# Attention scores in four quarters of TensorE, q and k loaded first, and a written order for the first block of a fused attention and expert kernel

## The chip, the cores and the metric

The kernel runs on one core of a Trainium2 chip. The metric is device time in microseconds (us). Before the change it is 997.73 us, the median of 3 runs (997.62 to 998.29).

## The reference

Three stages follow each other; all arrays are float32.

```
scores = q_c @ k_c^T / 8          # 4 batches x 8 heads x 9 chunks of 64 tokens, head size 64
attn   = softmax(scores)          # with the row's maximum taken off first
x      = (attn @ v_c) -> [2304 tokens, 512]
h      = x @ w_in;  g = h * clip(h + 3, 0, 6) / 6;  x2 = g @ w_out        # d_ff = 2048
logits = x2 @ w_gate;  noisy = logits + log1p(exp(x2 @ w_noise)) * noise  # 8 experts, top 2
out    = sum over the token's two experts of  weight * (relu(x2 @ w1[e]) @ w2[e])   # 1024 wide
```

## The kernel before

Tokens are cut into 18 tiles of 128; a tile holds two chunks of 64 tokens for all 8 heads. The middle stage runs in five blocks of 4, 4, 4, 3 and 3 tiles (`BT`, L28), and in each block over 16 units of 128 hidden channels (`U1`). Of a unit, `mlp_s1` (L294) makes the first product, 12 matmuls (L270), each weight and input being split into a high and a low part and three of the four products taken; `mlp_act` (L301) and `mlp_lo` (L309) make `g` (ScalarE L304, VectorE L305, ScalarE L306, VectorE L311); `mlp_o` (L313) makes the second product, 3 matmuls per tile (L279), one unit later. The experts' stage follows with 64 more units.

**Ticks.** TensorE's order is written by hand: after every 4 matmuls of a first product and every 3 (a tile) of a second one, `tick` (L259) runs the work that was put down for that number with `at`. A unit has 7 ticks in blocks of 4 tiles, 6 in blocks of 3. Attention of block b+1 and the gate of block b-1 are placed into block b in this way (L688 to L709). From block 0 on, the order of VectorE, ScalarE and SyncE (SP, which issues the loads) is left to a scheduler that works with its own estimates of durations.

**Weights.** Those of the middle stage arrive as 64-bit numbers. A unit has two halves (first and second product), 32 halves in all. `load64(s)` (L123) loads 512 KB for a half; `conv_u` (L133) takes three VectorE operations (L142, L143, L144) to put the float32 bits together; `conv_hi` (L148) makes the high part on ScalarE (L152), `conv_lo` (L154) the low part on VectorE (L159). They run during block 0, two halves per unit (L641). From half 14 on, three buffers are in use: `conv_u(s)` issues the load of half s+3.

**Attention of a tile.** `att_sc` (L164) makes the scores in 16 matmuls of 64 x 64 (32 instructions, L171): rows of the array hold one of two groups of heads (`r`), and each writes the same half of the output partitions, into one bank of PSUM. `att_mx` (L174) takes the maximum (L177) and subtracts it (L183), or, with `acts`, only scales it (L181) for `att_e` (L186), which then takes one exp per head with the maximum as bias and the sum as an extra output (L191), else one exp for all (L193). `att_n` (L195) sums if needed (L198), and multiplies by the inverse (L199, L200, L201). `att_pt` (L210) transposes on TensorE (L214), `att_at` copies (L218), `att_xo` (L225) makes the products with v (L235) in four quarters of the array and two banks, `att_hi` and `att_lo` split the result into the block's input, `Xa` or `Xb` (ScalarE L245, VectorE L248).

**PSUM.** `pairs` (L53) are two tiles of two banks each: pair 0 holds banks "p6" and "p7", pair 1 "p2" and "p5". Scores go to p6, transposes to p7, value products to the left half of both banks of pair 0, the gate's `gate_t`, `gate_m`, `gate_r` (L336 to L360) to p7. The second product uses p0, p1, p2 and p5.

**Before block 0** (L602 to L620) the order on TensorE, VectorE and ScalarE is written by hand: attention of tiles 0 to 3 and the first two halves of weights, with `keep_warm` (L545) matmuls on constants between. The loads are issued in the order tile 0 (three parts), tiles 1 to 3, halves 0 to 6 (L557). `constants` (L563) and `table_init` (L573) set up small tables, the latter at unit 6 of block 0.

## Time and profile before

| | |
|---|---|
| median of 3 runs | 997.73 us (997.62 to 998.29) |
| profiled execution: its own time, span | 996.98 us, 995.2 us |
| TensorE (PE) busy | 955.8 us, 96% of the span |
| its weight loads (PEld) busy | 811.2 us, 82% |
| VectorE (DVE) busy | 433.6 us, 44% |
| ScalarE (ACT) busy | 338.9 us, 34% |
| GpSimd (POOL) busy | 141.7 us, 14% |
| loads and stores | 99.47 MB, 100 GB/s on average |

A profile is one execution. Engines are PE (matmuls), PEld (their weight loads, beside PE), DVE, ACT, POOL and SP; L171 is line 171 of the kernel; `pair<-arena` is what an instruction writes and reads, by the program's names; x32 counts instructions. Matmuls are pipelined, and the ends that a profile gives them are modelled: how long a group takes on PE is better read from its start to the start of the next group. PEclk is the granted share of TensorE's clock.

### The profile page before, as it was taken

The numbers are of one execution on the slowest core, as the hardware profiler recorded it, in microseconds if no ns is written. First come the engines' busy times: TensorE is split into PE (matmuls) and PEld (weight loads), VectorE is DVE, ScalarE is ACT, GpSimd is POOL, SyncE is SP. The second block draws the span as 40 slices with busy tenths as digits, with TensorE's granted clock in tenths as the row PEclk, the third lists the DMA queues.
The fourth block names the chain that finished last, engine by engine and source line by source line (L and its number), as shares of the span: only waits on it lengthen the run. The fifth ranks groups of instructions, "written<-read, shape, count | busy, mean of one in ns | idle before, by whom it ended". The sixth has DMA issues, their size and how long they took to land.

```text
span 995.2 us, 14562 instructions
## 1 busy us (share of the span) xinstructions
PE 955.8 (96%) x5980; PEld 811.2 (82%) x5980; DVE 433.6 (44%) x863; ACT 338.9 (34%) x661; POOL 141.7 (14%) x129
## 2 busy tenths in 40 slices
PE   6898799999999999999999999999999999999995
PEld 4676687777777788878988899898998999899894
DVE  4999824344433434336542543434333343422221
ACT  4454433323333233335541433333333333321110
POOL 0000000000200020032103321301313130130311
PEclk8899899999999999999999999999999999999998
DMA  9536312011651021013541663644636354340422
GB/s 341 161 129 216 130 32 75 32 33 32 231 189 36 1 85 33 22 33 86 179 139 22 170 154 95 130 110 114 131 106 138 96 127 117 85 54 22 53 25 33
DMA packets 37196, 99.47 MB, mean 100 GB/s; under 512 B 9984, under 2 KB 10368, under 8 KB 37120
## 3 DMA queue, kind: packets, MB, share of 16 engines
q1 hardware_dynamic: 27008, 77.43, 24.0%
q0 software_dynamic: 10112, 21.02, 11.8%
q8 instruction: 49, 0.80, 0.3%
q14 instruction: 27, 0.22, 0.1%
HBM read 75.15 MB, written 23.28 MB: 99 GB/s over the span
## 4 chain that ended last, share of the span: by engine, by line
PE 87%; DVE 8%; DMA 2%; issue 1%; ACT 1%; POOL 0%; SPq 0%; DVEq 0%; ACTq 0%; POOLq 0%
PE h L270 41%; PE acc L279 21%; PE pair L279 19%; PE pair L453 2%; DMA raw<-in_w1u_dram 2%; DVE u L144 1%; DVE u L143 1%; PE pair L340 1%; PE pair L171 1%; DVE u L142 1%; PE pair L235 1%; DMA lead<-in_qkv_dram 1%; DVE g L311 1%; DVE r L305 1%; PE pair L349 1%
## 5 line engine op out<-in xcount | busy, mean ns | idle before, releaser
L279 PE MATMUL acc<-w,g 128*128 128x512 f32 x960 | 262.4, 398 | 2.5 <-DVE g L311 2.3
L270 PE MATMUL h<-Xa,w 128*128 128x320 f32 (+3 forms) x1344 | 251.7, 337 | 1.8 <-DVE Xa L248 1.7
L279 PE MATMUL pair<-w,g 128*128 128x512 f32 x864 | 235.3, 400 | 0.8 <-ACT at L341 0.8
L270 PEld LDWEIGHTS h<-Xa,w 128*128 128x128 f32 x1344 | 217.0, 189 | 22.7 <-DVE Xa L248 2.0
L279 PEld LDWEIGHTS acc<-w,g 128*128 128x128 f32 x960 | 174.3, 188 | 35.2 <-DVE g L311 3.2
L279 PEld LDWEIGHTS pair<-w,g 128*128 128x128 f32 x864 | 161.5, 190 | 38.3 <-ACT at L341 1.3
L119 DVE TENSOR_TENSOR w<-raw,w 128x1024 fp32r<-128x1024 f32 x64 | 78.4, 1226 | 132.6 <-ACT w L118 132.4
L470 DVE SCALAR_TENSOR_TENSOR g<-h,g 128x320 fp32r<-128x320 f32 (+2 forms) x128 | 62.5, 489 | 154.8 <-ACT g L469 145.4
L469 ACT ACTIVATE g<-h 128x320 fp32r<-128x320 f32 (+2 forms) x128 | 56.0, 438 | 191.6 <-PE h L270 186.4
L270 PE MATMUL h<-Xe,w 128*128 128x320 f32 (+1 forms) x672 | 110.2, 315 | 0.0
L270 PE MATMUL h<-Xb,w 128*128 128x384 f32 (+1 forms) x480 | 106.6, 366 | 0.0
L305 DVE SCALAR_TENSOR_TENSOR r<-r,h 128x512 f32<-128x512 f32 (+1 forms) x80 | 50.6, 632 | 126.4 <-ACT r L304 117.5
L270 PEld LDWEIGHTS h<-Xe,w 128*128 128x128 f32 x672 | 103.5, 188 | 2.5
L118 ACT ACTIVATE w<-raw 128x1024 fp32r<-128x1024 f32 x64 | 67.8, 1060 | 104.8 <-PE pair L279 97.1
L304 ACT ACTIVATE r<-h,b 128x512 f32<-128x512 f32 (+1 forms) x80 | 51.7, 646 | 151.9 <-PE h L270 150.7
L426 POOL DMA_INDIRECT table<-pay,slot x36 | 36.6, 1017 | 413.1 <-DVE slot L423 403.6
L270 PEld LDWEIGHTS h<-Xb,w 128*128 128x128 f32 x480 | 85.6, 188 | 11.1 <-issue 0.8
L443 POOL DMA_INDIRECT xr<-x2d,tab x40 | 39.3, 981 | 271.0 <-PE pair L453 252.1
L491 POOL DMA_INDIRECT out_dram<-arena,tab x40 | 63.1, 1576 | 88.0 <-DVE arena L488 69.7
L311 DVE TENSOR_TENSOR g<-r,g 128x512 fp32r<-128x512 f32 (+1 forms) x80 | 50.9, 636 | 32.9 <-ACT g L306 31.6
L306 ACT ACTIVATE g<-r 128x512 fp32r<-128x512 f32 (+1 forms) x80 | 47.2, 590 | 44.1 <-DVE r L305 43.1
L152 ACT ACTIVATE w<-u 128x512 fp32r<-128x512 f32 x32 | 19.7, 635 | 22.8 <-DVE u L144 22.7
(134 smaller groups left out, 525.8 us busy)
## 6 DMA issues: line engine op xcount, KB each, us to landing
raw<-in_w2u_dram SPq DMA_DIRECT2D x64, 512.0 KB, 3.9
raw<-in_w1u_dram SPq DMA_DIRECT2D x24, 512.0 KB, 4.1
arena<-in_qkv_dram SPq DMA_DIRECT2D x14, 768.0 KB, 4.2
out_dram<-zero SPq DMA_DIRECT2D x4, 1536.0 KB
rawx<-in_w1u_dram SPq DMA_DIRECT2D x8, 512.0 KB, 13.4
x2d<-x SPq DMA_DIRECT2D x15, 256.0 KB
lead<-in_qkv_dram SPq DMA_DIRECT2D x3, 768.0 KB
x2d<-zero SPq DMA_DIRECT2D x1, 1536.0 KB
```

The lines of the kernel that those rows point to most:

```text
L118: nc.scalar.activation(w[:, 0], raw, AF.Copy)
L119: nc.vector.tensor_tensor(w[:, 1], raw, w[:, 0].bitcast(F32), op=ALU.subtract)
L270: nc.tensor.matmul(dst, w[:, a, kd * P:(kd + 1) * P], x[:, b, kd, t0:t0 + n], start=(k == 0), stop=(k == 3 * KD - 1))
L279: nc.tensor.matmul(acc[i], g[:, a, i * P:(i + 1) * P], w[:, b, DM:], start=(first and j == 0), stop=(last and j == 2))
L304: nc.scalar.activation(r, st["h", b], AF.Relu, bias=b3)
L305: nc.vector.scalar_tensor_tensor(r, r, 6.0, st["h", b], op0=ALU.min, op1=ALU.mult)
L306: nc.scalar.activation(st["g", b, u][:, 0], r, AF.Copy)
L311: nc.vector.tensor_tensor(g[:, 1], st["r", b], g[:, 0].bitcast(F32), op=ALU.subtract)
L443: nc.gpsimd.indirect_dma_start(out=xr, out_offset=None, in_=x2d[:rows], in_offset=bass.IndirectOffsetOnAxis(ap=st["tab", key][:, i, 0:1], ...
L469: nc.scalar.activation(g[:, 0, t0:t0 + n], h, AF.Relu)
L470: nc.vector.scalar_tensor_tensor(g[:, 1, t0:t0 + n], h, 0.0, g[:, 0, t0:t0 + n].bitcast(F32), op0=ALU.max, op1=ALU.subtract)
L491: s = nc.gpsimd.indirect_dma_start(out=out, out_offset=bass.IndirectOffsetOnAxis(ap=tab[:, i, 0:1], axis=0), in_=y, in_offset=None, comput ...
```

## The change

- `att_sc` writes chunk `c` to one half of the partitions and head group `r` to one of two banks, so that four quarters of the array are addressed in turn. Scores and value products use the left (or, for tiles 2 and 3, the right) half of both banks of a pair, transposes the right half of pair 0.
- `att_n` is divided: `att_r` (sum, inverse) and the multiplication; `att_ns` does the multiplication head by head on ScalarE. `conv_u` is divided into `conv_1` (L142, L143) and `conv_2` (L144 and the next load).
- q and k of tiles 0 to 3 are loaded first, then v with the weights. `constants` and `table_init` stand before the attention of tiles 0 to 3, whose order is written anew, with 27 warm matmuls in place of 30 and three halves of weights converted in place of two.
- Block 0 becomes `block0`, in which the order on TensorE, VectorE and ScalarE is written; a tile of attention is spread over four units (28 ticks), with the exps and the multiplications on ScalarE, four heads at a time.
- In blocks 1 to 3 the transposes come 6 ticks (5 in block 3) behind the scores instead of 11, the value products 4 ticks behind these as before, and the gate's three steps behind the value products instead of between scores and transposes.

The diff, cut to its core:

```diff
-    def load_tile(t, buf, parts=1):
-        n = 3 * DM // parts
-        for i in range(parts):
-            nc.sync.dma_start(buf[:, i * n:(i + 1) * n], qkv[:, t, i * n:(i + 1) * n])
+    def load_part(t, buf, i0, i1):
+        nc.sync.dma_start(buf[:, i0 * DM:i1 * DM], qkv[:, t, i0 * DM:i1 * DM])
+
+    def load_tile(t, buf, whole=True):
+        if whole:
+            load_part(t, buf, 0, 3)
...
-    def conv_u(s):
+    def conv_1(s):
         if s >= 2 * U1:
             return
         j, h = divmod(s, 2)
         if h == 0:
             st["w", "m", j] = wpool.tile([P, 2, 2 * DM], F32R, tag="w", bufs=U1, name="w")
-        raw = st.pop(("raw64", s)).rearrange("p (n c) -> p n c", c=2)
-        lo32, hi32 = raw[:, :, 0], raw[:, :, 1]
+        raw = st["raw64", s].rearrange("p (n c) -> p n c", c=2)
+        hi32 = raw[:, :, 1]
         u = work.tile([P, DM], I32, tag="x2", bufs=3, name="u")
         nc.vector.tensor_scalar(u, hi32, 3, 0x3fffffff, op0=ALU.logical_shift_left, op1=ALU.bitwise_and)
         nc.vector.scalar_tensor_tensor(u, hi32, -0x40000000, u, op0=ALU.bitwise_and, op1=ALU.bitwise_or)
+        st["u", s] = u
+
+    def conv_2(s):
+        if s >= 2 * U1:
+            return
+        lo32 = st.pop(("raw64", s)).rearrange("p (n c) -> p n c", c=2)[:, :, 0]
+        u = st["u", s]
         nc.vector.scalar_tensor_tensor(u, lo32, 29, u, op0=ALU.logical_shift_right, op1=ALU.bitwise_or)
-        st["u", s] = u
         load64(s + 7 if s < 10 else s + 3 if s >= 14 else -1)
...
-    def att_sc(t, tag):
+    def att_sc(t, pair=0, half=0):
         qt, kt, vt = st["qkv", t]
-        sc = bank(tag, [P, 8, 64], "sc")
-        for c in range(2):
-            for hp in range(KD):
+        sc = pairs[pair][:, :, half * 2 * P:(half + 1) * 2 * P].rearrange("p r (h k) -> p r h k", h=KD)
+        for hp in range(KD):
+            for c in range(2):
                 for r in range(2):
                     s = slice(r * 64, r * 64 + 64)
-                    nc.tensor.matmul(sc[s, c * KD + hp, :], qt[s, hp, c, :], kt[s, c, hp, :], start=True, stop=True)
+                    nc.tensor.matmul(sc[c * 64:c * 64 + 64, r, hp, :], qt[s, hp, c, :], kt[s, c, hp, :],
+                                     start=True, stop=True)
         st["sc", t] = sc
...
     def att_mx(t, acts):
         sc = st["sc", t]
-        mx = work.tile([P, 8, 1], F32, tag="mx", bufs=2, name="mx")
-        nc.vector.tensor_reduce(mx, sc, axis=AX.X, op=ALU.max)
+        mx = work.tile([P, 8, 1], F32, tag="mx", bufs=4, name="mx")
+        mx4 = mx.rearrange("p (r h) o -> p r h o", r=2)
+        nc.vector.tensor_reduce(mx4, sc, axis=AX.X, op=ALU.max)
         sm = (lead[t][:, 3 * DM:] if t < BT[0] else arena[:, 6]).rearrange("p (h k) -> p h k", h=8)
...
-    def att_e(t):
+    def att_e(t, heads=range(8)):
         sm, su, mx, acts = st["att", t]
-        sc = st.pop(("sc", t))
         if acts:
-            for h in range(8):
-                nc.scalar.activation(sm[:, h], sc[:, h], AF.Exp, scale=0.125, bias=mx[:, h], accum_out=su[:, h])
+            sc = st["sc", t]
+            for h in heads:
+                nc.scalar.activation(sm[:, h], sc[:, h // KD, h % KD], AF.Exp, scale=0.125, bias=mx[:, h],
+                                     accum_out=su[:, h])
...
+    def att_r(t):
         sm, su, mx, acts = st["att", t]
         if not acts:
             nc.vector.tensor_reduce(su, sm, axis=AX.X, op=ALU.add)
         nc.vector.tensor_scalar(su, su, 1e-9, None, op0=ALU.add)
         nc.vector.reciprocal(su, su)
+
+    def att_n(t):
+        att_r(t)
+        sm, su, mx, acts = st["att", t]
         nc.vector.tensor_tensor(sm, sm, su.to_broadcast([P, 8, 64]), op=ALU.mult)
-    def att_a(t, tag, acts):
-        att_sc(t, tag)
+    def att_ns(t, heads):
+        sm, su, mx, acts = st["att", t]
+        for h in heads:
+            nc.scalar.activation(sm[:, h], sm[:, h], AF.Copy, scale=su[:, h])
+
+    def att_a(t, acts):
+        att_sc(t)
...
-    def att_pt(t, tag):
+    def att_pt(t, tag=None):
         sm = st.pop(("att", t))[0].rearrange("p h k -> p (h k)")
-        pt = bank(tag, [P, KD, P], "pt")
+        if tag is None:
+            pt = pairs[0][:, :, 2 * P:].rearrange("p r (j n) -> p r j n", j=2)
+        else:
+            pt = bank(tag, [P, KD, P], "pt").rearrange("p (r j) n -> p r j n", r=2)
...
-    def att_xo(t, pair=0):
+    def att_xo(t, pair=0, half=0):
-                                         at[s, c * 2 + j, r * 64:r * 64 + 64], start=True, stop=True)
+                                         at[s, r * 2 + j, c * 64:c * 64 + 64], start=True, stop=True)
...
-    for c in [0, 1, 2, 3, 10, 11, 12, 13, 14, 15, 16]:
-        if c < 10:
-            load_tile(c, bufs[c], 3 if c == 0 else 1)
-        else:
-            load64(c - 10)
+    for t in range(4):
+        for i in ((0, 1), (1, 2)) if t == 0 else ((0, 2),):
+            load_part(t, bufs[t], *i)
+        load_tile(t, bufs[t], False)
+    load_part(0, bufs[0], 2, 3)
+    load_part(1, bufs[1], 2, 3)
+    load64(0)
+    load_part(2, bufs[2], 2, 3)
+    load_part(3, bufs[3], 2, 3)
+    for i in range(1, 7):
+        load64(i)
...
+    constants()
+    table_init()
+    LT = BT[0]
     with tc.manual_schedule(engines={nc.tensor.engine, nc.vector.engine, nc.scalar.engine}):
-        att_sc(0, "p0"), att_mx(0, True), att_e(0)
-        att_sc(1, "p1"), att_mx(1, True), att_e(1)
+        att_sc(0, 0, 0), att_mx(0, False), att_e(0)
+        att_sc(1, 1, 0), att_mx(1, True), att_e(1)
+        att_n(0)
+        keep_warm(1)
+        att_sc(2, 0, 1), att_mx(2, True)
+        att_sc(3, 1, 1), att_pt(0, "p0"), att_at(0, at_[0]), att_e(2)
+        att_mx(3, False), att_e(3)
+        att_n(1)
+        keep_warm(1)
+        att_xo(0, 0, 0), att_hi(0)
+        att_pt(1, "p1"), att_at(1, at_[1])
+        att_n(2), att_n(3)
         keep_warm(3)
-        att_n(0), att_pt(0, "p3"), att_at(0, at_[0])
-        att_sc(2, "p0"), att_mx(2, True)
-        keep_warm(3)
-        att_n(1), att_e(2), att_pt(1, "p3"), att_xo(0, 0), att_at(1, at_[1])
-        att_sc(3, "p1"), att_mx(3, False)
-        att_hi(0), att_e(3), att_xo(1, 1)
-        keep_warm(6)
-        conv_u(0)
-        att_lo(0), att_hi(1), conv_hi(0), att_n(2), att_n(3)
-        att_pt(2, "p3"), att_at(2, at_[0]), att_pt(3, "p3"), att_at(3, at_[1])
-        att_lo(1), att_xo(2, 0), att_xo(3, 1)
-        keep_warm(8)
-        conv_u(1), att_hi(2), conv_hi(1), att_hi(3)
-        conv_lo(0), conv_lo(1)
-        att_lo(2), att_lo(3)
-    constants()
-    LT = BT[0]
+        att_pt(2, "p0"), att_xo(1, 1, 0), att_pt(3, "p1")
+        conv_1(0), conv_2(0), conv_hi(0)
+        att_hi(1), att_lo(0)
+        att_at(2, at_[0]), att_at(3, at_[1])
+        att_xo(2, 0, 1), att_xo(3, 1, 1)
+        att_hi(2), att_hi(3)
+        att_lo(1), conv_lo(0), att_lo(2), att_lo(3)
+        keep_warm(12)
+        conv_1(1), conv_2(1), conv_hi(1)
+        conv_1(2), conv_2(2), conv_hi(2)
+        conv_lo(1), conv_lo(2)
...
-            if b == 0:
-                for s in (2 * u + 2, 2 * u + 3):
-                    conv_u(s)
-                    conv_hi(s)
-                    conv_lo(s)
...
+    def block0():
+        nonlocal prev
+        n0 = st.get("tick", 0)
+        for i in range(4):
+            k = n0 + 28 * i
+            t = LT + i
+            at(ticks, k + (3 if i == 0 else 1), att_sc, t)
+            at(ticks, k + 3 * 7 - 4 + 1, att_pt, t)
+            at(ticks, k + 3 * 7 + 3, att_xo, t)
+        for u in range(U1):
+            t, k = LT + u // 4, u % 4
+            mlp_s1(0, u, gtile(), 0)
+            mlp_act(0, u)
+            if k == 3:
+                att_at(t, at_[0])
+            for pb, v in prev:
+                mlp_o(pb, v)
+            prev = [(0, u)]
+            if k == 1:
+                att_e(t, range(4, 8))
+            elif k == 2:
+                att_ns(t, range(4, 8))
+            b, a = 2 * u + 3, 2 * u + 4
+            conv_1(b)
+            mlp_lo(0, u)
+            conv_2(b)
+            conv_hi(b)
+            if k == 0:
+                att_mx(t, True)
+                att_e(t, range(4))
+            elif k == 1:
+                att_r(t)
+                att_ns(t, range(4))
+            elif k == 3:
+                att_hi(t)
+                if t + 2 < NTILE:
+                    load_tile(t + 2, bufs[4 + t % 2])
+            conv_1(a)
+            conv_2(a)
+            conv_hi(a)
+            conv_lo(b)
+            if k == 3:
+                att_lo(t)
+            conv_lo(a)
...
+    with tc.manual_schedule(engines={nc.tensor.engine, nc.vector.engine, nc.scalar.engine}):
+        block0()
     order = tc.manual_schedule(engines={nc.tensor.engine})
     order.__enter__()
-    for b in range(NB):
+    for b in range(1, NB):
         side = {}
-        if b == 0:
-            at(side, 6, table_init)
         n0 = st.get("tick", 0)
         every = 24 if BT[b] == 4 else 20
-        if 0 < b < NB - 1:
+        if b < NB - 1:
             t0, nt = GRP[b - 1]
             for i in range(nt):
-                n = n0 + 8 + every * i
+                n = n0 + every - 4 + every * i
                 at(ticks, n, gate_t, t0 + i, "p7")
                 at(ticks, n + 4, gate_m, t0 + i, "p7")
                 at(ticks, n + 7, gate_r, t0 + i, "p7")
             at(ticks, n + 8, gate_top, b - 1)
-            at(ticks, n + 22, gate_pos, b - 1)
+            at(ticks, n + 18, gate_pos, b - 1)
         if b == 2:
             at(side, 1, zero_out)
         if b + 1 < NB:
             for i in range(BT[b + 1]):
                 t = B0[b + 1] + i
                 n = n0 + 6 + every * i
-                at(ticks, n, att_a, t, "p6", b == 0)
-                at(ticks, n + 11, att_b, t, "p7")
-                at(ticks, n + 15, att_c, t)
+                at(ticks, n, att_a, t, False)
+                at(ticks, n + (6 if every > 20 else 5), att_b, t)
+                at(ticks, n + (10 if every > 20 else 9), att_c, t)
                 if t + 2 < NTILE:
-                    at(ticks, n + 16, load_tile, t + 2, bufs[4 + t % 2])
+                    at(ticks, n + 11, load_tile, t + 2, bufs[4 + t % 2])
         if b == NB - 2:
             for j in range(3):
                 at(side, 12 + j, load_raw, U1 + j)
```

## Rows read from the trace of the kernel before

**Rows 1.** The page's 40 slices: busy tenths of VectorE.
```profile
DVE  4999824344433434336542543434333343422221
```
**Rows 2.** Stretches: length, busy PE, PEld, DVE, ACT, POOL, PEclk, DMA share, GB/s.
```profile
5.40:20.00 14.60, 11.14 (x203) 7.93 (x206) 4.71 (x13) 8.88 (x51) 0.00 (x0) 0.77 0.99 388
...
25.00:30.00 5.00, 4.25 (x73) 3.22 (x73) 4.90 (x11) 2.26 (x4) 0.00 (x0) 0.50 0.29 116
...
34.40:107.00 72.60, 61.04 (x392) 47.15 (x392) 69.54 (x134) 36.72 (x97) 0.76 (x3) 0.97 0.50 164
107.00:147.50 40.50, 40.26 (x252) 32.39 (x253) 20.98 (x38) 15.02 (x36) 0.00 (x0) 0.93 0.23 75
147.50:252.00 104.50, 104.28 (x712) 81.41 (x711) 42.26 (x100) 32.72 (x57) 4.72 (x5) 1.00 0.13 41
```
**Rows 3.** Timeline of PE: the first product of block 1 starts.
```profile
147.45 0.86 PE L270 MATMUL h<-Xb,w 128*128 128x512 f32 x3
```
**Rows 4.** Chain that ended last, 128 to 153 us: start, us, what.
```profile
131.55 0.44 PE pair L214 x4
...
135.01 0.62 PE pair L235 x32
...
139.26 1.39 PE acc L279 x6
...
142.06 2.76 PE h L270 x12
...
152.51 1.08 PE pair L171 x32
```
**Rows 5.** Who waited for whom on PE, 0 to 147.5 us: total, times, longest.
```profile
PE pair L214 <- DVE arena L201: 9.3, 3, 4.8
...
PE acc L279 <- DVE g L311: 2.3, 2, 1.7
```
**Rows 6.** Chain that ended last, 34 to 60 us: conversions back to back.
```profile
53.84 0.67 DVE u L142 x2
54.51 1.80 DVE u L143 x3
```
**Rows 7.** Timeline: attention of one tile in block 2, one in block 3.
```profile
257.93 0.95 PE L279 MATMUL pair<-w,g 128*128 128x512 f32 x3
258.05 0.69 DVE L177 TENSOR_REDUCE mx<-pair 128x8 f32<-128x512 f32 x1 [0.33 <-PE pair L171]
...
258.77 0.69 DVE L183 TENSOR_TENSOR arena<-pair,mx 128x512 f32<-128x512 f32 x1
...
261.32 0.69 DVE L201 TENSOR_TENSOR arena<-arena,su 128x512 f32<-128x512 f32 x1
...
376.90 1.66 PE L270 MATMUL h<-Xb,w 128*128 128x384 f32 x8
...
381.39 0.69 DVE L201 TENSOR_TENSOR arena<-arena,su 128x512 f32<-128x512 f32 x1
```
**Rows 8.** Line L191 in a stretch: length, busy ACT, PEclk, DMA share, GB/s.
```profile
8.20:10.70 2.50, 2.47 (x16) 0.89 1.01 393
```
**Rows 9.** Timeline: scores of tiles 0 and 1.
```profile
5.45 1.72 PE L171 MATMUL sc<-lead 64*64 64x64 f32 x32
9.16 1.18 PE L171 MATMUL sc<-lead 64*64 64x64 f32 x32 [2.00 <-DMA lead<-in_qkv_dram]
```
**Rows 10.** Who waited for whom on PE, 147.5 to 434.7 us.
```profile
PE pair L340 <- DVE arena L183: 0.9, 3, 0.4
```
**Rows 11.** The page's DMA issues; who waited in SP's queue, 0 to 150 us.
```profile
raw<-in_w1u_dram SPq DMA_DIRECT2D x24, 512.0 KB, 4.1
...
SPq L103 <- PE pair L235: 31.0, 3, 20.9
```
**Rows 12.** Timeline: value product and its readers in block 3.
```profile
407.49 0.69 PE L235 MATMUL pair<-at,arena 64*64 64x64 f32 x32
...
408.88 0.69 DVE L248 TENSOR_TENSOR Xa<-pair,Xa 128x512 fp32r<-128x512 f32 x1 [1.01 <-ACT Xa L245]
```
**Rows 13.** Line L214 in a stretch: length, busy PE, PEld, PEclk, DMA share, GB/s.
```profile
12.40:13.50 1.10, 1.03 (x4) 0.72 (x4) 0.50 1.02 417
```

More of the change, by code (lines that the diff above doesn't have):

```diff
@@ L175, in att_mx @@
         sc = st["sc", t]
-        mx = work.tile([P, 8, 1], F32, tag="mx", bufs=2, name="mx")
-        nc.vector.tensor_reduce(mx, sc, axis=AX.X, op=ALU.max)
+        mx = work.tile([P, 8, 1], F32, tag="mx", bufs=4, name="mx")
+        mx4 = mx.rearrange("p (r h) o -> p r h o", r=2)
+        nc.vector.tensor_reduce(mx4, sc, axis=AX.X, op=ALU.max)
         sm = (lead[t][:, 3 * DM:] if t < BT[0] else arena[:, 6]).rearrange("p (h k) -> p h k", h=8)
-        su = work.tile([P, 8, 1], F32, tag="su", bufs=2, name="su")
+        su = work.tile([P, 8, 1], F32, tag="su", bufs=4, name="su")
         if acts:
@@ L182, in att_mx @@
         else:
-            nc.vector.tensor_tensor(sm, sc, mx.to_broadcast([P, 8, 64]), op=ALU.subtract)
+            nc.vector.tensor_tensor(sm.rearrange("p (r h) k -> p r h k", r=2), sc,
+                                    mx4.to_broadcast([P, 2, KD, 64]), op=ALU.subtract)
+            st.pop(("sc", t))
         st["att", t] = (sm, su, mx, acts)
-    def att_e(t):
+    def att_e(t, heads=range(8)):
         sm, su, mx, acts = st["att", t]
-        sc = st.pop(("sc", t))
         if acts:
-            for h in range(8):
-                nc.scalar.activation(sm[:, h], sc[:, h], AF.Exp, scale=0.125, bias=mx[:, h], accum_out=su[:, h])
+            sc = st["sc", t]
+            for h in heads:
+                nc.scalar.activation(sm[:, h], sc[:, h // KD, h % KD], AF.Exp, scale=0.125, bias=mx[:, h],
+                                     accum_out=su[:, h])
         else:
             nc.scalar.activation(sm, sm, AF.Exp, scale=0.125)
-    def att_n(t):
+    def att_r(t):
         sm, su, mx, acts = st["att", t]
@@ L207, in att_a, with att_b @@
         att_n(t)
-    def att_pt(t, tag):
+    def att_pt(t, tag=None):
         sm = st.pop(("att", t))[0].rearrange("p h k -> p (h k)")
-        pt = bank(tag, [P, KD, P], "pt")
+        if tag is None:
+            pt = pairs[0][:, :, 2 * P:].rearrange("p r (j n) -> p r j n", j=2)
+        else:
+            pt = bank(tag, [P, KD, P], "pt").rearrange("p (r j) n -> p r j n", r=2)
         for m in range(KD):
-            nc.tensor.transpose(pt[:, m, :], sm[:, m * P:(m + 1) * P], ident)
+            nc.tensor.transpose(pt[:, m // 2, m % 2], sm[:, m * P:(m + 1) * P], ident)
         st["pt", t] = pt
     def att_at(t, at):
-        nc.scalar.activation(at, st.pop(("pt", t)), AF.Copy)
+        nc.scalar.activation(at.rearrange("p (r j) n -> p r j n", r=2), st.pop(("pt", t)), AF.Copy)
         st["attT", t] = at
-    def att_b(t, tag):
-        att_pt(t, tag)
+    def att_b(t):
+        att_pt(t)
         att_at(t, at_[0])
-    def att_xo(t, pair=0):
+    def att_xo(t, pair=0, half=0):
         at = st.pop(("attT", t))
         qt, kt, vt = st.pop(("qkv", t))
-        xo = pairs[pair][:, :, :2 * P].rearrange("p a (j n) -> p a j n", j=2)
+        xo = pairs[pair][:, :, half * 2 * P:(half + 1) * 2 * P].rearrange("p a (j n) -> p a j n", j=2)
         for c in range(2):
```

## The prediction

> **What bounds the kernel now.** I read the slices first, then the busy time by stretch, then who waited for whom on TensorE, then single durations. In the slices VectorE is full only in the first tenth of the run [rows 1]. The stretches say it sharply: from 34.4 to 107 us VectorE is busy 69.5 of 72.6 us, TensorE 61.0; from 107 to 147.5 TensorE has 40.3 of 40.5 and VectorE half; in the next block TensorE has 104.3 of 104.5 [rows 2]. So block 0, which ends where the first product with Xb starts, at 147.45 [rows 3], is held up by VectorE in its first part, and everything behind it by TensorE. How much is lost there: TensorE's own work in block 0 is 16 first products of 2.76, 15 second products of 1.39 + 1.40 (the two halves have the same row) and 4 tiles of attention at 1.08 (scores) + 0.44 (transposes) + 0.62 (values) [rows 4]: 44.2 + 41.9 + 8.6 = 94.7 us. It takes 113 us, from 34.4 to 147.45: some 18 lost. The largest wait is that of the transposes for the normalised softmax on VectorE, 9.3 us in three waits; then g, 2.3 [rows 5]. VectorE is not short of work then, it does the wrong work first: the scheduler lets weight conversions run ahead of what TensorE waits for.
>
> **Part 1, the order up to the first product.** I walk along the written order with durations of rows. VectorE: 0.60 us from one 512-element operation to the next, 0.34 for L142 [rows 6]; 0.72 where the next one reads the result, as 258.05 to 258.77 [rows 7]. ScalarE: 0.58 for a copy (an estimate, from VectorE's step for as many elements), 2.47 for eight exps of a tile [rows 8]. The scores of tile 0 start at 5.45 as now; those of tile 1 start at 9.16 now, behind 1.5 MB of loads [rows 9]. With q and k alone 1.0 MB is ahead: 0.5 MB less at 388 GB/s [rows 2], so 7.8. Exp of tile 0 at 8.0, the eight exps of tile 1 from 9.8 to 12.2. Score 3 then writes the other half of a pair that these exps still read. I take it that it waits for them: today a gate transpose into one bank of a pair waits for L183, which reads only the other bank [rows 10]. So score 3 at 12.2, transposes of tile 0 at 13.2, their copy 14.2 to 14.8, eight exps of tile 2 to 17.1, exp 3 to 17.7, two more copies to 19.8. VectorE has normalised tiles 2 and 3 by 20.0 and converts the first half to 21.8. Four copies on ScalarE (weights, tile 1, two transposed tiles) to 24.2, the last two value products and copies to 26.4, the last L248 to 27.0. The 12 warm products run from 25.6 to 29.2 and the first unit behind them to 31.9. Meanwhile VectorE converts halves 1 and 2, 27.0 to 32 (2 x 2.14, and a few 0.1 where a step reads the one before). Unit 1 starts on TensorE at 32.8.
>
> Hidden: the constants and the table's start (about ten short operations on VectorE and GpSimd, now before 5.45, where both engines wait for the first load; were that cover gone, some 1.5 us); their three loads go behind the weights on SP's queue, and 0.3 MB more ahead of later ones is 0.8 us on weights that arrive at least 5 us early. The warm products go from 30 to 27 and stay off the chain except the last 12.
>
> **Part 2, block 0.** Per four units, which hold one tile of attention, VectorE does 8 halves x (0.34 + 3 x 0.60) = 17.1, L305 and L311 8 x 0.60 = 4.8, and for the tile the maximum, the scaling, two short ones and L248, 1.8. The normalising multiplication, 0.60, goes to ScalarE as eight small ones, 1.6 to 2.5 us there per tile; ScalarE is busy 36.7 of 72.6 us now [rows 2], so it has room. In the written order some steps read the one just before (0.12 each), and the last subtraction of a unit waits 0.2 for ScalarE's copy: another 1.9. Sum 25.6 us. TensorE's own: 4 x (2.76 + 2.79) + 0.62 + 0.44 + 0.62 + 0.6 for changing between shapes = 24.5. So VectorE sets the pace, just. Unit 2 waits for its weights behind the first body of VectorE, 7.1 us after unit 1, at 39.9; unit 13 follows 11 units, or 2.75 x 25.6 + 2 (its turn of attention) later, at 112.4; from there VectorE has nothing left to convert, and three units with their attention take 18.8. Block 1 starts at **131.2** instead of 147.45: **-16.2**. The shorter scores save nothing here: VectorE covers them, and if it did not, they would be 1.8.
>
> VectorE now waits in its written order for each load of weights, with L305, L311 and the softmax queued behind the wait. A load lands 4.1 us after its issue (median) [rows 11]; with three buffers it is issued three halves, about 7 us, ahead. At nothing, then. In SP's queue it stands behind the load of an attention tile, which waits for a value product; that is a rival.
>
> **Part 3, scores in four quarters, blocks 1 to 3.** Unmeasured; bounds are 1.08 (two quarters at a time, as now) and 0.62, what the value product of the same shapes takes, which already uses four quarters and two banks [rows 4]. I take 0.62, the same pattern. Ten tiles: **-4.6** (bound 0). The Trainium skill, TensorE: Matmul & The Clock Gate, section "Wait — 56ns, not 53.3ns?", says that two matmuls never start less than about 25 ns apart; by that 32 of them would take 0.80, and ten tiles save 2.8. The row disagrees: 0.62 for 32 is 19 ns each.
>
> **Part 4, the shorter distances there.** Now the transposes come 11 ticks behind the scores and the gate lies between; then 6 (blocks 1, 2) or 5 (block 3), the gate behind the values. The chain is scores, L177, L183, exp, L198, two short ones, L201. Undisturbed it takes from TensorE's next product (257.93) to the end of L201 (261.32 + 0.69) 4.1 us; with the unit's own work between, 376.90 to 382.08, 5.2 [rows 7]. Six ticks are one first product and three to four quarters of a second, 4.7 to 5.0: about 0.1 a tile over seven tiles, **+0.7**. Five ticks of block 3, whose products are 0.70 per tick, are 3.6: 0.5 to 1.6 a tile, **+3.0** for three. There the gate's transposes also come one tick (0.8) behind the value product, in its bank, which is free when L248 has read it: 407.49 to 409.57 is 2.08 [rows 12], less 0.62 is 1.46. So 0.7 each, **+2.2**. The gate's own waits behind L183 go: **-0.9** [rows 10]. The routing of these blocks comes 6 us later, far ahead of its first reader in block 4; loads of later tiles come 5 ticks earlier, harmless. Bounds of the part: -0.9 and +9 (every tile at 5.2).
>
> **Sum** -16.2 - 4.6 + 0.7 + 3.0 + 2.2 - 0.9 = -15.8. The profiled execution took 996.98 us (span 995.2): 981.2. The median of the runs is 997.73, 0.75 above it: **982.0**.
>
> **The rivals.**
> *TensorE paces block 0.* If the small waits of VectorE (1.9 in 25.6) don't appear, it needs 23.7, under TensorE's 24.5, and the block ends near 124.5; with no new stall behind, -23 - 5.5, **969**. Against it: steps that read the one before cost 0.12 in the rows.
> *TensorE at half rate.* It idles more in the first 30 us. Today four transposes there take 1.03 at a granted clock of 0.50, 1.2 GHz [rows 13], against 0.44; from 25 to 30 us it is 0.50 again [rows 2]. If the 12 warm products and unit 0 run so, unit 1 comes 3 to 6 us later: up to **988**. For it: half as many short bursts as now. Against it: twelve in a row just before. The same page of the Trainium skill, section "What's actually happening", has the clock fall when the engine idles; by that rule it is 988. The trace shows both levels in this stretch, so it keeps a chance.
> *Scores not faster.* If the four quarters do not overlap, the change does not do what it says: -4.6 goes and 1.4 in the first part is added: **988**.
> *SP blocked: the other side.* A load of an attention tile waits on SP for the value product (31.0 us in three waits now, the longest 20.9 [rows 11]), and the weights' loads stand behind it. Should it be queued before them, VectorE, in order, stops for the same time. Three such loads lie among the conversions; the kernel is slower from 5.3 us each (15.8 / 3), and with 7 each takes 982 + 21 = **1003**. Against it: in the written order the load comes after the value product has been read, so its wait should be about nothing.
>
> **How the numbers follow.** Forecast 0.60 (its own range 977 to 986: part 4's bounds at half, and 2 us of loads); TensorE paces 0.15; half rate 0.12; scores not faster 0.06; SP blocked 0.07, of which slower 0.04, the same 0.02, faster 0.01. 0.2%, 2 us, is about what a measurement of this kernel can tell from no change. Range 973 to 989: it takes in both 988 cases and, above 973, a third of the 969 case; some 0.16 is left out. Faster 0.94, same 0.02, slower 0.04.
>
> **What would show it.** Right: block 1's first product near 131; VectorE busy over 95% from 27 to 120; scores at 0.62; no wait over 2 us on TensorE in block 0; transposes in block 3 waiting for L201, about 1 us each. Wrong: waits of VectorE for the weights' loads; a granted clock of 0.5 after 28 us; scores at 1.08; gate transposes waiting in blocks 1 and 2.

## The result, and the profile after

The change makes the kernel **slower**: 1003.12 us (median of 5 runs, 1000.66 to 1003.62) against 997.62, a ratio of 1.0052 (95% interval 1.0036 to 1.0068): half a per cent, small but clear of the noise. Forecast were 982.0 us, 973 to 989. The profiled execution has a span of 1001.8 us, before 995.2.

The busy time by stretch shows where. The stretches are the blocks, from the first product of one to that of the next (columns as in [rows 2], with the counts of instructions behind the busy times).

```profile
28.60:133.56 104.96, 99.34 (x644) 75.95 (x645) 97.52 (x177) 61.08 (x167) 0.00 (x0) 0.98 0.45 144
133.56:236.74 103.18, 102.87 (x711) 79.50 (x712) 42.73 (x100) 32.80 (x57) 0.00 (x0) 1.00 0.15 49
236.74:344.25 107.51, 102.42 (x644) 79.89 (x643) 38.61 (x94) 31.00 (x54) 8.89 (x9) 0.97 0.29 106
344.25:437.94 93.69, 81.68 (x598) 68.41 (x597) 33.88 (x94) 27.72 (x54) 8.19 (x9) 0.96 0.12 38
437.94:515.09 77.15, 74.02 (x390) 64.63 (x389) 40.81 (x83) 38.05 (x60) 16.76 (x17) 0.98 0.37 112
```

Block 1 starts at 133.56 instead of 147.45 [rows 3]: the lead and block 0 gain 13.9 us. Block 1 takes 103.18 (before 104.49). Then the gain is lost and more: block 2 takes 107.51 (before 101.29), block 3 93.69 (81.47), block 4 77.15 (74.69); the rest takes 486.7 us instead of 485.8. In these stretches TensorE is no longer full: 5 us are idle in block 2, 12 in block 3 and 3 in block 4. Who waited for whom on TensorE, 133 to 520 us (total, times, longest):

```profile
PE pair L239 <- DVE arena L218: 14.6, 4, 6.8
PE pair L374 <- issue: 2.6, 1, 2.6
PE pair L365 <- DVE Xa L273: 2.0, 3, 0.9
```

The transposes (L239) wait for the normalised softmax as they did in block 0 before [rows 5]. That alone looks like the short distance that the prediction priced at 0.5 to 1.6 us a tile. The timeline of the start of block 2 tells another story:

```profile
241.02 9.22 SPq L358 DMA_DIRECT2D x2d<-x  x3
...
241.68 0.69 PE L179 MATMUL pair<-arena 64*64 64x64 f32 x32
241.82 0.96 POOL L451 DMA_INDIRECT table<-pay,slot  x1 [0.30 <-issue]
...
243.12 2.90 PE L295 MATMUL h<-Xa,w 128*128 128x512 f32 x12
...
246.90 0.96 POOL L451 DMA_INDIRECT table<-pay,slot  x1 [0.30 <-issue]
247.85 0.98 POOL L626 MEMSET zero<- 128x1024 f32 x1
247.88 0.69 DVE L187 TENSOR_REDUCE mx<-pair 128x8 f32<-128x512 f32 x1 [5.33 <-remote]
...
249.29 0.60 ACT L357 ACTIVATE x<-pair 128x512 f32<-128x512 f32 x1 [7.47 <-remote]
...
252.43 1.12 PE L239 MATMUL pair<-ident,arena 128*128 128x128 f32 x4 [5.01 <-DVE arena L218]
```

The softmax itself is not slow. Its maximum (L187) needs only the scores, which TensorE has finished by 242.4, and it starts at 247.88; "remote" says that nothing in the trace ended where it was released. ScalarE's copy of the third tile (L357), which waits for a second product, is as late. TensorE goes on with the next products meanwhile: it works, but its releases (the signals that tell another engine that a result is ready) arrive 5 to 6 us late. In that time GpSimd issues the routing's scatter (L451, eight indirect DMAs, 237.80 to 247.86), which `gate_pos` starts; group 0 is the routing of block 0's tiles, group 1 that of block 1's, group 2 that of block 2's. Before the change group 0's scatters ran from 246.06 to 256.88, across the start of block 2 (251.94), and the last was issued at 255.91, just ahead of the first tile's scores (256.85); now the first is issued 1 us behind the block's start. In block 1, which no scatter precedes, nothing is late. In block 3 the delay is longer still, 6.9 us from the end of the scores to the maximum:

```profile
348.56 0.69 PE L179 MATMUL pair<-arena 64*64 64x64 f32 x32
...
356.11 0.69 DVE L187 TENSOR_REDUCE mx<-pair 128x8 f32<-128x512 f32 x1 [6.98 <-remote]
```

Nor is waiting all of it. During each stop, or just behind it, TensorE's granted clock falls, and the products that follow run at the lower of its two levels, 1.2 GHz, for a while:

```profile
251.00:257.50 6.50, 5.07 (x14) 4.20 (x15) 2.56 (x6) 1.17 (x2) 0.00 (x0) 0.50 1.01 382
357.00:363.50 6.50, 3.08 (x10) 2.60 (x11) 3.75 (x8) 2.22 (x4) 0.00 (x0) 0.50 0.73 246
449.00:452.00 3.00, 3.00 (x14) 2.12 (x14) 1.34 (x3) 1.16 (x3) 0.00 (x0) 0.50 0.00 0
```

### The profile page after: what moved, and what is told of

Its sections match the earlier page's. It is cut to its first block, busy times and chain, and to the rows that moved or that the text cites. A ratio compares the mean times of both kernels' runs of the same rounds, so it can differ in the third digit from the quotient of the medians.

```text
span 1001.8 us, 14548 instructions
## 1 busy us (share of the span) xinstructions
PE 951.7 (95%) x5977; PEld 803.4 (80%) x5977; DVE 436.6 (44%) x860; ACT 345.2 (34%) x678; POOL 140.4 (14%) x129
## 4 chain that ended last, share of the span: by engine, by line
PE 81%; DVE 11%; ACT 3%; issue 2%; another core or an unknown queue 1%; DMA 1%; POOL 0%; SPq 0%; ACTq 0%; POOLq 0%
PE h L295 38%; PE acc L304 19%; PE pair L304 18%; DVE u L153 2%; PE pair L478 2%; DVE u L145 1%; DVE r L330 1%; DVE g L336 1%; DVE w L167 1%; PE pair L365 1%; DVE u L144 1%; PE pair L239 1%; ACT w L160 1%; PE pair L260 1%
## 5 line engine op out<-in xcount | busy, mean ns | idle before, releaser
L295 PE MATMUL h<-Xa,w 128*128 128x320 f32 (+3 forms) x1344 | 254.8, 338 | 2.0 <-ACT w L160 1.8
L451 POOL DMA_INDIRECT table<-pay,slot x36 | 35.2, 978 | 494.6 <-DVE slot L448 485.1
```

What stands on the lines that cost most here:

```text
L295: nc.tensor.matmul(dst, w[:, a, kd * P:(kd + 1) * P], x[:, b, kd, t0:t0 + n], start=(k == 0), stop=(k == 3 * KD - 1))
```

## The experiments

The **theory** from here on: the loss is the scatter, which `gate_pos`, moved 8 ticks later (4 in block 3), now puts onto the next block's start. The **rival**: the short distances alone. All ratios below are to runs of the kernel before on the same chip.

**e1.** The scatters of tiles 0 to 11 are left out.
```diff
-        for t in range(t0, t0 + nt):
+        for t in range(t0, t0 + nt if g >= 3 else t0):
             for k in range(2):
                 s = nc.gpsimd.indirect_dma_start(
```


> Edit: the kernel after without the 24 routing scatters (L451) of tiles 0 to 11; the routing table of these tiles keeps its first values, so the experts' rows are wrong. Theory (the scatter, moved 8 ticks later, now lies on the start of the next block, and while it runs beside the block's stores TensorE's semaphore reaches VectorE and ScalarE 5 us late): the first tiles of blocks 2 and 3 lose their stops of 6 to 8 us and the start of block 4 its 2 us; 986 to 989 us. Rival (the short distance between scores and transposes alone makes TensorE stop): the scatter has nothing to do with it, 1001 to 1004 us, and the first transposes of blocks 2 and 3 still wait 5 us or more.

982.24 us, ratio 0.9839 (0.9818 to 0.9859): the theory holds, and more than expected is gained. Timeline at the same place, and what is left of TensorE's waits from 133 to 520 us:

```profile
240.53 0.69 PE L179 MATMUL pair<-arena 64*64 64x64 f32 x32
241.32 0.68 DVE L187 TENSOR_REDUCE mx<-pair 128x8 f32<-128x512 f32 x1
```
```profile
PE pair L239 <- DVE arena L218: 3.9, 3, 1.4
PE pair L365 <- DVE Xa L273: 2.0, 3, 0.9
```

The maximum follows the scores at once. What remains are the three tiles of block 3, 1.3 us each for the transposes and 0.7 for the gate (forecast 1.0 and 0.7). The blocks of e1 from the second to the fourth show the clock at 1.00 throughout and TensorE less busy than in the kernel after (102.42, 81.68 and 74.02 us there), 5.8 us in all:

```profile
235.58:335.40 99.82, 99.74 (x643) 78.05 (x642) 38.68 (x94) 31.20 (x54) 0.00 (x0) 1.00 0.31 114
335.40:421.41 86.01, 80.11 (x599) 67.23 (x597) 34.05 (x94) 27.85 (x54) 0.00 (x0) 1.00 0.13 41
421.41:494.55 73.14, 72.50 (x391) 63.65 (x389) 40.74 (x83) 38.14 (x60) 10.41 (x9) 1.00 0.39 117
```

**e2.** Only the move of `gate_pos`, in the kernel before.
```diff
-            at(ticks, n + 22, gate_pos, b - 1)
+            at(ticks, n + (30 if every > 20 else 26), gate_pos, b - 1)
```


> Edit: the kernel before with gate_pos of blocks 1 to 3 at the ticks it has after the change (110, 110 and 94 from the block's start, instead of 102, 102 and 90), nothing else. Theory (scatter beside the start of the next block makes TensorE's semaphore late): VectorE's maximum of the first tile in blocks 2 and 3 starts several us after its scores; with 11 ticks of distance and the gate's transposes in between, part of it is still covered, so 1 to 5 us slower than before, 999 to 1003 us. Rival (short distances alone): no difference from before, 997 to 998 us, and the maximum starts as soon as the scores are done.

1015.30 us, ratio 1.0182 (1.0162 to 1.0202): slower by more than expected, and the rival falls. Eleven ticks cover nothing, since the gate's transposes between scores and transposes wait for the same late softmax. TensorE's waits, 147 to 527 us:

```profile
PE pair L340 <- DVE arena L183: 13.0, 5, 6.5
PE pair L349 <- ACT at L341: 2.7, 1, 2.7
```

**e3, e4.** e3 keeps the short distances and brings `gate_pos` back to the tick it had; e4 takes blocks 1 to 3 from the kernel before.
```diff
-        every = 24 if BT[b] == 4 else 20
+        every, gate0 = (22, 18) if BT[b] == 4 else (18, 16)
...
-                n = n0 + every - 4 + every * i
+                n = n0 + gate0 + every * i
```


> Edit: the kernel after with 22 ticks between tiles (18 in block 3) instead of 24 (20), and the gate right behind the value products, so that gate_pos comes at tick 102 (88 in block 3), where it was before the change or earlier, with the same short distances in each tile. Theory (scatter beside the start of the next block): the stops of the first tiles of blocks 2 and 3 and at the start of block 4 go, the waits of about 1 us in block 3 stay; 985 to 990 us. Rival (short distances alone): the stops of 5 us and more stay at the first tiles, 1000 to 1005 us.

> Edit: the kernel after up to the end of block 0, with blocks 1 to 3 as before (scores in two quarters at a time and one bank, 11 ticks to the transposes, the gate between, gate_pos at tick 102). Theory: all of the gain lies ahead of block 1 and all of the loss in blocks 1 to 4, so this gives the 13.9 us by which block 1 starts earlier: 983 to 985 us. Rival (part of the lead is given back later whatever blocks 1 to 3 look like, for instance because the experts' stage waits for weights or for the routing): 988 us or more.

e3: 989.03 us, 0.991 (0.9891 to 0.9929). e4: 984.13 us, 0.9864 (0.9845 to 0.9883). Both times are as the theory expects. The 5 us stops need the late scatter, though one stop of 2.3 us, expected to go, stays in e3 at the start of block 4, where group 2's scatters still run. The lead is not given back: e4's block 1 starts 15.3 us earlier than before, and 12.9 of that is left at the end.

**e5.** Meant to put the x2 stores behind the scatters.
```diff
+            if b in (1, 2):
+                at(ticks, st["tick"] + 11, x2_store, t, x2)
...
```


> Edit: the kernel after with the scatters where they are, but the stores of x2 at the start of blocks 2 and 3 put down 11 ticks later, behind the end of the scatters. If it is scatters beside stores that make TensorE's semaphore late: the stops of 6 to 8 us at the first tiles of blocks 2 and 3 go, 986 to 991 us (the start of block 4 keeps its own). If the scatters do it alone: the stops stay, 1000 to 1004 us.

1001.69 us, 1.004 (1.0026 to 1.0054), and it tells nothing: SP's order is left to the scheduler, which put the stores where they had been, among the scatters (235.94 to 246.03): the first two at 239.15 and 239.95.

**e6, e7.** The scatters of groups 0 and 1 into the next block, beside its second tile of attention; e7 also has block 3 as before.
```diff
-            at(ticks, n + 18, gate_pos, b - 1)
+            if b < 3:
+                at(ticks, n0 + 112 + 28, gate_pos, b - 1)
+            else:
+                at(ticks, n + 18, gate_pos, b - 1)
```


> Edit: the kernel after with gate_pos of groups 0 and 1 put into the next block, 28 ticks behind its start, so that the scatters run far from the x2 stores but beside the second tile of attention (block 2 has the stores of zeros there, block 3 has none). If it takes stores beside the scatters: block 3 is free of stops of over 2 us, block 2 may keep one beside the zeros; 986 to 991 us. If any score or transpose beside a scatter is released late: the stop of 5 us or more moves to the second tile in both blocks, 999 to 1004 us.

> Edit: the kernel after with block 3 as before the change (scores in two quarters, 11 ticks to the transposes, the gate between), gate_pos of groups 0 and 1 in the next block (tick 28 of block 2, tick 24 of block 3), that of group 2 at tick 90 of block 3. Theory (the scatter's place is the loss, the short distances in block 3 cost 4 us, four quarters save 1.3 to 1.5 us in blocks 1 and 2): 980 to 983 us, faster than both kernels. Rival (a scatter beside a tile of attention stops TensorE wherever it lies): 990 us or more.

e6: 996.71 us, 0.9991 (0.9979 to 1.0002); e7: 985.28 us, 0.9871 (0.9854 to 0.9888). Both lie between the two cases expected, so neither case fits. The delay needs no stores: in e6's block 3, where none run, the value product is read 6 us late and the gate stops TensorE for 6.7, while the transposes just ahead are read at once:

```profile
366.56 0.66 PE L239 MATMUL pair<-ident,arena 128*128 128x128 f32 x4 [1.29 <-DVE arena L218]
...
367.26 0.60 ACT L243 ACTIVATE at<-pair 128x512 f32<-128x512 f32 x1 [2.50 <-PE pair L239]
...
369.95 0.69 PE L260 MATMUL pair<-at,arena 64*64 64x64 f32 x32
...
374.24 0.97 POOL L451 DMA_INDIRECT table<-pay,slot  x1 [0.30 <-issue]
376.87 0.60 ACT L270 ACTIVATE Xa<-pair 128x512 fp32r<-128x512 f32 x1 [5.73 <-remote]
...
378.25 1.11 PE L365 MATMUL pair<-ident,x 128*128 128x128 f32 x4 [6.71 <-DVE Xa L273]
```

In block 2 the same place costs 2 us (101.89 against 99.82 in e1). So the cost depends on which release falls into the scatter's time, and not every release there is late.

**e8 to e11.** e8 has block 3 as before and puts the scatters on a stretch of plain products. e9 asks what they cost before the change. e10 and e11 replace them by plain writes of as many small rows, from SP (second diff) and from GpSimd (the same with `nc.gpsimd`).
```diff
...
+            at(ticks, n + 22 if b == 3 else n0 + 112 + 77, gate_pos, b - 1)
...
```
```diff
...
+                nc.sync.dma_start(dump[(2 * t + k) * P:(2 * t + k + 1) * P, :], slot[:, t, :])
...
```


> Edit: block 3 as before the change, and gate_pos of groups 0 and 1 at tick 77 of the next block, where for about 14 ticks TensorE runs nothing but the plain first and second products. Theory (a scatter holds up TensorE only where scores, transposes or value products stand beside it): block 1 takes 103.2 us, block 2 99.8, as without scatters, block 3 81.7 as with the old order; 979 to 982 us. Rival (a scatter costs 2 to 3 us wherever it is put): 984 to 987 us.

> Edit: the kernel before without the 24 routing scatters of tiles 0 to 11 (the experts' rows are wrong). How much the scatters cost before the change: theory (little, since they lie on plain products, except that of group 2 at the start of block 4): 1 to 3 us faster than before, 994 to 997 us. Rival (the scatters cost as much before as after): 980 to 984 us.

> Edit: the kernel after with the 24 scatters of tiles 0 to 11 replaced by 24 plain writes of as many bytes in as many rows (128 rows of 8 bytes each), issued on SP's queue behind the same VectorE results, to a tensor that nothing reads (the experts' rows are wrong). If the small writes themselves hold back TensorE's releases: stops at the first tiles of blocks 2 and 3 stay, 996 us or more. If it is GpSimd's making of the scatters: 982 to 986 us, as without scatters.

> Edit: the same 24 plain writes, issued on GpSimd's queue. If GpSimd's making of the descriptors holds back TensorE's releases, indirect or not: the stops stay, 996 us or more. If only the indirect form does it: 982 to 987 us.

e8: 977.85 us, 0.9827 (0.9808 to 0.9846). e9: 996.03, 1.0008 (0.9996 to 1.002). e10: 982.23, 0.987 (0.9848 to 0.9893). e11: 982.76, 0.9876 (0.9854 to 0.9898). Read alone, they say that plain writes are harmless and that the scatters cost nothing before. But in e8 the scatters of group 2 run to 424.65, over the start of block 4 (416.24), and there nothing is late:

```profile
419.87 0.97 POOL L466 DMA_INDIRECT table<-pay,slot  x1 [0.30 <-issue]
...
421.29 0.66 PE L380 MATMUL pair<-ident,x 128*128 128x128 f32 x4
...
421.99 0.60 ACT L381 ACTIVATE at<-pair 128x512 f32<-128x512 f32 x1 [0.75 <-PE pair L380]
```

These four ran on another chip than the runs so far, and their traces differ in one more thing. The DMA issues of the kernel after, then of e8 (the last number is the median time from issue to landing):

```profile
table<-pay,slot POOLq DMA_INDIRECT x36
```
```profile
table<-pay,slot POOLq DMA_INDIRECT x36, 2.4
```

The profile gives no time to landing where landing events are missing. Each DMA leaves 16 of them: of the 384 of the scatters of tiles 0 to 11 the trace of the kernel after holds 115, that of the kernel before 223, that of e8 all 384. All traces with late releases lack some; those of e8 to e11 lack none. So e8, e10 and e11 were run again beside the kernel after, on one chip.

> The kernel after, unchanged, on the chip of this call. If the chip is one whose traces lack the landing events of the indirect DMAs: 1000 to 1004 us, with stops of 6 to 8 us at the first tiles of blocks 2 and 3. If it is one that shows them: no release is late, no stop over 2 us there, and the change does what was forecast, 981 to 986 us.

> e8 unchanged, beside f1. On a chip with late releases: block 2 in 99.8 to 100.2 us, block 3 in 81.2 to 81.8, and the start of block 4 loses 2 to 4 us to group 2's scatters, 979 to 982 us. On one without: 977 to 979 us.

> e11 unchanged (24 plain writes of 128 rows of 8 bytes on GpSimd's queue for the scatters; the experts' rows are wrong), beside f1. If f1 has the stops and the indirect form alone makes them: 981 to 985 us. If any small writes that GpSimd issues make them: 996 us or more. If f1 has no stops, it tells nothing: 981 to 985 us.

> e10 unchanged (the same writes on SP's queue; the experts' rows are wrong), beside f1. If f1 has the stops and the small writes themselves make them: 996 us or more; if not: 981 to 985 us.

This chip is of the first sort (landings missing). f1: 1002.55 us, 1.0037 (1.0024 to 1.0051), with the stops. f3: 982.88, 0.9848 (0.9828 to 0.9869) and f4: 981.83, 0.9832 (0.9813 to 0.985), without. TensorE's longest waits from 133 to 520 us in f1, then in f3:

```profile
PE pair L239 <- DVE arena L218: 15.2, 4, 7.6
```
```profile
PE pair L240 <- DVE arena L219: 3.9, 3, 1.4
```

On one chip, then, the scatters stop TensorE and plain writes of as many rows, even from GpSimd, don't. The two also differ in length, though. In f3 GpSimd issues the eight writes of group 0 in 4.5 us and is done just ahead of the end of the scores that are late in f1:

```profile
235.66 4.53 POOL L452 DMA_DIRECT2D dump<-slot  x8 [233.41 <-DVE slot L449]
...
240.14 0.69 PE L180 MATMUL pair<-arena 64*64 64x64 f32 x32
...
240.93 0.68 DVE L188 TENSOR_REDUCE mx<-pair 128x8 f32<-128x512 f32 x1
```

Their last landing event is at 247.16, so writes under way don't hold up a release. Whether it is the indirect form, or the 10 us that GpSimd spends on it, f3 does not separate.

f2 is a miss: 988.06 us, 0.9895 (0.9876 to 0.9915). Blocks 2 and 3 came as expected, but group 2's scatters, queued behind group 1's, cost block 4 not 2 to 4 us but 10.6:

```profile
416.32 2.27 PE L310 MATMUL h<-Xa,w 128*128 128x384 f32 x12
...
421.90 2.93 PE L319 MATMUL acc<-w,g 128*128 128x512 f32 x6 [3.31 <-ACT g L346]
...
427.32 0.58 ACT L344 ACTIVATE r<-h,b 128x384 f32<-128x384 f32 x1 [5.47 <-remote]
427.80 0.59 ACT L372 ACTIVATE x<-acc 128x512 f32<-128x512 f32 x1
...
429.58 1.12 PE L380 MATMUL pair<-ident,x 128*128 128x128 f32 x4 [3.27 <-ACT x L372]
```

The first of these waits is that of a plain second product, and a plain first product that ended at 418.59 is read from 427.32, 8.7 us late: plain products are a better place, not a safe one.

**e12.** One line of the kernel after.
```diff
-            at(ticks, n + 18, gate_pos, b - 1)
+            at(ticks, n + 18 if b == 3 else n0 + 112 + (77 if b == 1 else 64), gate_pos, b - 1)
```


> Edit: the kernel after with one line changed: gate_pos of group 0 at tick 77 of block 2 and that of group 1 at tick 64 of block 3, behind the last value product and on plain products; group 2 stays at tick 94 of block 3, right ahead of block 4. If the place of the scatters is the whole error of the prediction: block 2 takes 99.8 to 100.5 us and block 3 86 to 87 (its short distances remain), block 4 keeps the 3 to 4 us of group 2's scatter; 984 to 988 us. If the scatters only explain part of it: 990 us or more.

986.59 us, 0.9879 (0.986 to 0.9897), as the theory expects, on a chip whose traces lack the landings. Blocks 2 to 4:

```profile
235.12:334.98 99.86, 99.78 (x643) 78.04 (x642) 38.81 (x93) 31.19 (x54) 8.11 (x8) 1.00 0.31 114
334.98:421.13 86.15, 80.25 (x600) 67.24 (x599) 34.74 (x97) 27.84 (x54) 8.18 (x9) 1.00 0.14 41
421.13:498.04 76.91, 73.89 (x390) 64.49 (x389) 40.74 (x83) 38.13 (x60) 17.10 (x17) 0.98 0.38 111
```

**g1, g2.** e7 with the last gates of blocks 2 and 3 moved up, so that the scatters of groups 0 and 1 end inside block 2 and those of group 2 soon behind block 3; e4 beside it.
```diff
...
+                n = n0 + {1: (20, 44, 68, 92), 2: (20, 44, 66, 75), 3: (8, 28, 48, 64)}[b][i]
...
+            at(ticks, n0 + {1: 112 + 82, 2: 96, 3: 86}[b], gate_pos, b - 1)
...
```


> Edit: e7 (blocks 1 and 2 as after, block 3 as before the change) with the last tiles' gates of blocks 2 and 3 moved up, behind the last value product, and gate_pos of group 0 at tick 82 of block 2, of group 1 at tick 96 of block 2, of group 2 at tick 86 of block 3: the scatters of groups 0 and 1 end ahead of block 3, those of group 2 end 3 us behind its end instead of 7. If the place decides: block 2 in 99.8 to 100.5 us, block 3 in 81.2 to 82, 979 to 982 us. If sixteen scatters in a row hold TensorE up even on plain products: block 2 in 103 us or more, 984 us or more.

> e4 unchanged, beside g1 on one chip: 983 to 985 us, or about 981 if this chip's releases are not late.

g1: 979.49 us, 0.9833 (0.9819 to 0.9847); g2: 981.76, 0.9858 (0.9842 to 0.9874). The traces show the landings, so this chip is of the second sort and the question put to g1 stays open. e4 was thus measured on both sorts and is faster than the kernel before on both; the kernel after was run on the first sort only.

The length of each block in the profiled executions, us, from the first product of one to that of the next (late: the traces lack landings of the scatters):

| | block 1 | block 2 | block 3 | block 4 | late |
|---|---|---|---|---|---|
| before | 104.49 | 101.29 | 81.47 | 74.69 | yes |
| after | 103.18 | 107.51 | 93.69 | 77.15 | yes |
| e1, no scatter | 103.18 | 99.82 | 86.01 | 73.14 | yes |
| e2, before, gate_pos late | 104.49 | 108.82 | 89.34 | 77.20 | yes |
| e4, blocks 1 to 3 as before | 105.13 | 101.70 | 81.69 | 74.92 | yes |
| e12, one line | 103.05 | 99.86 | 86.15 | 76.91 | yes |
| f2 | 103.06 | 99.84 | 81.55 | 83.80 | yes |
| e8, the same kernel as f2 | 103.05 | 99.84 | 81.23 | 73.16 | no |
| g2, the same kernel as e4 | 105.14 | 101.33 | 81.14 | 73.16 | no |
| g1 | 103.07 | 100.29 | 81.08 | 73.16 | no |

## Why the prediction was wrong

**The step that failed** is one sentence of part 4: "The routing of these blocks comes 6 us later, far ahead of its first reader in block 4", costed at nothing. It asked only who reads what the moved step writes. What the step does while it runs was not asked: its 24 scatters, which had run across the boundary of two blocks, moved 4 to 8 ticks later, onto the start of the next one. The price is after less e1, block by block: 107.51 - 99.82 = 7.7, 93.69 - 86.01 = 7.7, 77.15 - 73.14 = 4.0, together 19.4 us. Before paid some of it, 74.69 - 73.14 = 1.55 in block 4, so the change added about 17.8. e2, which makes this move alone, loses as much in blocks 2 to 4: 7.5 + 7.9 + 2.5 = 17.9. Of the 19.4, 5.8 are TensorE's products at the lower clock, the rest is idle time. In the profiled executions (forecast 981.2, measured 1003.62) this leaves some 4.6 us: 2.4 by which block 1 starts later than forecast, 1.4 in the other terms of blocks 1 to 3, 0.9 behind block 4. e1, the change without these scatters, takes 982.24, all but the 982.0 forecast; that is in part luck, since it also saves the 1.55 that the kernel before pays. The sum also left GpSimd's queue out of part 4 altogether, although it named SP's.

The trace of before had the sign, in a stretch that was not read. Group 2's scatters lay on the start of block 4 even then:

```profile
439.75 0.66 PE L340 MATMUL pair<-ident,x 128*128 128x128 f32 x4
...
440.71 0.96 POOL L426 DMA_INDIRECT table<-pay,slot  x1 [0.30 <-issue]
...
442.76 1.08 ACT L341 ACTIVATE at<-pair 128x512 f32<-128x512 f32 x2 [3.06 <-PE h L270]
```

Four transposes are done by 440.4, and ScalarE, idle, copies them 2.3 us later, 1.1 us behind the end of the last scatter. The releaser named there, a later product, only ended nearest to that time.

**Point by point.** Part 1 was right: unit 1 starts at 33.24 (forecast 32.8), and the granted clock from 25 to 30 us is 1.00 (before 0.50 [rows 2]), so the rival of half rate falls at the place that it named. A clock of 0.50 after 28 us, named as a sign of being wrong, did come, later:

```profile
50.00:52.50 2.50, 2.50 (x8) 1.91 (x7) 2.34 (x5) 1.23 (x2) 0.00 (x0) 0.50 0.57 193
```

Part 2 was right in its cause and 2.4 us short: VectorE is busy 89.44 of 93.0 us from 27 to 120; unit 2 starts at 40.08 (39.9); four units take 25.6 and 25.7 (25.6), so TensorE does not pace the block. The time is lost at the first tile of attention: the step from unit 3 to unit 4 takes 10.04 us, the same step of the next two tiles 8.09 and 8.17, and unit 13 starts at 114.25 instead of 112.4. In e1, where the clock stays at 1.00 there, that first step takes 9.15, so 0.9 of it is the clock. The start of block 1 differs from run to run: in the other 16 traces with this block 0 it lies between 130.90 and 132.69. VectorE waits for no load of weights, so SP blocked falls too: the loss came on that side, by another mechanism, which no rival named, and that this rival's price was 1003 is a coincidence.

Part 3 was right: ten tiles of scores take 0.62 us from their start to the next product. That is 19 ns for each of 32 matmuls. The Trainium skill, TensorE: Matmul & The Clock Gate, section "Wait — 56ns, not 53.3ns?", has no two matmuls start less than about 25 ns apart; the trace disagrees, as it did before the change. Part 4's other terms were right in kind: without scatters, blocks 1 and 2 gain 1.3 and 1.5 us (forecast together -3.2 + 0.7, and part of -0.9), and block 3 loses 4.5 (forecast -1.4 + 3.0 + 2.2 = 3.8): transposes 3.9 in three waits, gate 2.0. e8 and g2 give these 4.5 back by the old order there.

e12 is the test of the whole: with the routing moved and all else as in the change, 986.59 us, inside the forecast range. It is 4.6 us above the forecast, 3.8 of them in block 4, where group 2's scatters stayed (76.91 against 73.14).

## What to carry to other kernels

When a step moves, ask not only who reads its result but what it does to its neighbours at the new place, on every queue that it starts. Keep indirect DMAs off the stretches in which short TensorE groups are read at once by other engines; plain products are the better place (e12), with few scatters in a row (f2). Count a stop of TensorE with what the lower clock costs behind it. Where a wait ends on "remote", look at what GpSimd is doing, and where a gain is small, measure on more than one chip.

## What the runs showed of the hardware that was not expected

While eight indirect DMAs of 128 rows run on GpSimd's queue (10 us), TensorE's releases can reach VectorE and ScalarE several us late, though TensorE itself goes on: 6.2 us for the value product in e6 (ended 370.64, read from 376.87), 6.9 for the scores of block 3 in the kernel after, 8.7 for a first product in f2, behind sixteen in a row. VectorE and ScalarE release each other promptly in the same time (e6: L193 ends at 266.79, L206, which waits for it, starts at 266.82). No wait of over 0.3 us of TensorE, VectorE or ScalarE ends on "remote" later than 2.4 us behind a scatter of tiles 0 to 11, not even in the experts' stage with its 80 indirect DMAs. 24 plain writes of 128 rows of 8 bytes, from SP or GpSimd, have no such effect (f3, f4 beside f1), but they are issued in less than half the time.

It appears on some chips and not on others: f2 and e8 are one kernel, 988.06 and 977.85 us. Where it appears, the traces also lack landing events: most of the scatters' in the kernel after (115 of 384 are there) and some of the x2 stores' beside them (147 of 240; in e1, without the scatters, all 240). What holds the releases back is not settled by these runs. Every run here lists the profiler's span and clock, so none shows whether the recording itself takes part. Nor was the kernel after run on a chip without the effect, where e8's blocks suggest that it would come near its forecast.
